# Head pairs 4 to 7 projected in float32 from the loaded tiles, and a new list of gates for the weight conversions

## The chip, the core and the metric

The kernel runs on one core of one Trainium2 chip. The core has five engines that run side by side, each with its own in-order queue of instructions: TensorE (PE in the profile, with its weight loads as PEld) does matrix products, VectorE (DVE), ScalarE (ACT) and GpSimd (POOL) do elementwise work, and SyncE (SP) issues most of the transfers (DMAs). Results of TensorE land in PSUM, everything else lives in SBUF. The metric is the device time of one execution in microseconds (us), as the median of several runs.

## The reference

Eight batches, each with 8 heads of 576 tokens and 64 numbers per token and head, go through an attention with a feature map, and the result through a token mix and a channel mix.

```python
def phi(x):
    proj = np.einsum('bhsd,df->bhsf', x, w_phi)          # 64 -> 128 features
    proj = proj - np.max(np.abs(proj), axis=-1, keepdims=True)
    return np.concatenate([np.exp(proj), np.exp(-proj)], axis=-1)
q_p, k_p = (phi(q), phi(k))
kv = np.einsum('bhsf,bhsd->bhfd', k_p, v)
z = np.sum(k_p, axis=2)
num = np.einsum('bhsf,bhfd->bhsd', q_p, kv)
den = np.einsum('bhsf,bhf->bhs', q_p, z)[..., None] + 1e-06
x = (num / den), heads side by side                       # (8, 576, 512)
h = np.maximum(xt @ w_tok1, 0.0) @ w_tok2                 # xt: tokens last, 576 -> 256 -> 576
u = x + h.transpose(0, 2, 1)
h2 = np.maximum(u @ w_ch1, 0.0) @ w_ch2                   # 512 -> 1536 -> 512
return u + h2
```

## The kernel before, in words

A head pair is two neighbouring heads of a batch; there are 32, pairs 0 to 3 are batch 0, pairs 4 to 7 batch 1. For each pair `keys()` projects the keys in five groups (four of two 128-row units, one of a single unit), subtracts the largest absolute value of each row, takes both exponentials and adds their products with the values in PSUM (`add_kv`). `queries()` does the same projection for the queries in one tail unit and four groups, turns the result, takes the exponentials and forms numerators and denominators. The projections of one pair are 18 units: 9 for keys and 9 for queries.

A projection is done in one of two ways by `less_max`. For pairs below `PLAIN` (4) it is a float32 product of the loaded tile (keys in the lower, queries in the upper 64 partitions) with `wz`, the projection weights beside zeros, 128 columns; VectorE then reads the result in PSUM twice, for the maximum (L252) and for the subtraction (L254). From pair 4 on `stack` first makes of the loaded `raw` tile a float32r stack of a rounded part (VectorE cast, L212) and a remainder (GpSimd subtraction, L213), two pieces of 512 and 640 columns for the keys and two for the queries; one float32r product of 256 columns per unit (L238) gives two partial sums; ScalarE copies one out (L245), VectorE adds the other (L247) and takes the maximum from SBUF (L252), and GpSimd subtracts it (L254).

The large products are done in float32r with each operand split in a rounded part and a remainder, three products for one. The channel weights arrive as 64-bit floats: 12 pieces of `wc1` and 12 of `wc2`. `convert` turns one piece: a DMA into a `raw` tile (SyncE), an absolute value on ScalarE (L146), four VectorE instructions on the bits (L147 to L150, tiles `bitsc`), a rounding copy on ScalarE and a subtraction on GpSimd (L77). The first eight conversions are gated: `turn_of` lets conversion n be written into the program only when `GATES[n]` denominators of batch 0 exist, and a copy of one column by GpSimd (L145) makes it wait for that denominator (`dn`, L443) on the chip. Each pair of batch 0 gives two such denominators, so gates 0 and 1 belong to pair 0, 2 and 3 to pair 1, and so on. The channel mix of a block of 256 tokens (`h` up, `acc` down) starts on a piece of the weights when that piece is in `loaded`.

Five generators (keys, queries, token mix, weight loading, channel mix) are woven by shares (`weave`), and a scheduler then sets each engine's order with a timeline of its own when the program is built. On the chip each engine follows that order strictly.

Of the kernel before, what the change touches and what calls it, by code (L numbers as in the profile page):

```python
# [18 lines left out]
B, H, S, D = 8, 8, 576, 64  # L19
NP = H // 2  # L20
# [2 lines left out]
T = 256  # L23
E = 1536
NC_, NE, NT = C // P, E // P, T // P
PLAIN = 4
ROWS = 8
BURST = 8
GATES = [4, 4, 6, 6, 7, 7, 7, 7]
BORROWED = 18  # L30
STAGES = 4
LAST = 15
# [12 lines left out]
def mixer_kernel(ctx, tc, qk, vm, vt, w_phi, w1, w2, wc1, wc2d, out):  # L45
# [21 lines left out]
    def column(pool, n, **kw):  # L67

        return pool.tile([P, 32], F32, **kw)[:, :n]
# [45 lines left out]
    for j in range(2):  # L115
        t = cst.tile([P, 672], F32, name=f"v{j}")[:, :650].rearrange("p (u j d) -> p u j d", u=5, j=2)
# [39 lines left out]
    def turn_of():  # L156
# [3 lines left out]
        ngated[0] += 1  # L160
        g = GATES[min(n, len(GATES) - 1)]
        yield from until(lambda: len(gates) > g)
        return gates[g] if n < len(GATES) else None

# [40 lines left out]
    def stack(raw, base, name):  # L205

        out = []
        lo = D - base
        for k, (c, n) in enumerate(((0, 512), (512, 640))):
            t = wk.tile([P, n], F32R, tag=f"{name[0]}{k}", name=f"st{name}{k}", bufs=1)  # L210
            src = raw[base:base + D, c:c + n]
            nc.vector.tensor_copy(t[base:base + D], src)  # L212
            nc.gpsimd.tensor_tensor(t[lo:lo + D], src, t[base:base + D].bitcast(F32), op=ALU.subtract)  # L213
            out.append(t)
        return out

    def less_max(ts, units, name, base=None):

        n, kind = len(units), name[0]
        if base == D:
            ps = ps_a.tile([P, 2, 2, F], F32, tag=f"a{nplain['k'] % 2}", name=f"pp{name}")
            nplain["k"] += 1
        elif base == 0 and (nplain["q"] % 2 == 0 or nplain["q"] >= BORROWED):
            ps = ps_h.tile([P, 2, 2, F], F32, tag="h", name=f"pp{name}")
            nplain["q"] += 1
        elif base == 0:
            ps = ps_w.tile([P, 2, 2, F], F32, tag="keys", name=f"pp{name}", bufs=1)
            nplain["q"] += 1  # L230
        elif kind == "k":
            ps = ps_w.tile([P, 2, 2, F], F32, tag="keys", name=f"pp{name}", bufs=1)
        else:
            ps = ps_w.tile([P, 2, 2, F], F32, name=f"pp{name}", **REST)
        for i, u in enumerate(units):
            t, c = (ts[1], 512) if u is None else (ts[u[0]], P * u[1])
            if base is None:
                nc.tensor.matmul(ps[:, i].rearrange("p two f -> p (two f)"), t[:, c:c + P],  # L238
                                 wp2.rearrange("p two f -> p (two f)"), start=True, stop=True)
            else:  # L240
                rows = slice(D, P) if name == "k0_0" else slice(0, P)
                nc.tensor.matmul(ps[:, i, 0], t[rows, c:c + P], wz[rows, base // D], start=True, stop=True)
        if base is None:
            part = wk.tile([P, 2, F], F32, tag="part", name=f"part{name}")
            nc.scalar.copy(part[:, :n], ps[:, :n, 1])  # L245
            pr = wk.tile([P, 2, F], F32, tag="p", name=f"p{name}")
            nc.vector.tensor_tensor(pr[:, :n], ps[:, :n, 0], part[:, :n], op=ALU.add)  # L247
            pr, eng = pr[:, :n], nc.gpsimd
        else:
            pr, eng = ps[:, :n, 0], nc.vector  # L250
        mx = column(wk, 2, tag=f"mx{kind}", name=f"mx{name}")
        nc.vector.tensor_reduce(mx[:, :n], pr, axis=AX.X, op=ALU.max, apply_absolute_value=True)  # L252
        pm = wk.tile([P, 2, F], F32, tag=f"pm{kind}", name=f"pm{name}", bufs=1 if kind == "t" else 2)
        eng.tensor_tensor(pm[:, :n], pr, mx[:, :n].unsqueeze(2).to_broadcast([P, n, F]), op=ALU.subtract)  # L254
        return pm

    nplain = {"k": 0, "q": 0}
    raws, pairs, kvs, loaded = {}, {}, {}, set()
    asked, attended, mixed = set(), set(), set()

    def load(i):

        raw = wk.tile([P, 2 * S], F32, tag="raw", name=f"raw{i}", bufs=1)
        lo, hi = (D if i <= PLAIN else 0), (D if i == B * NP else P)
        nc.sync.dma_start(raw[lo:hi], qk[i, lo:hi])
        raws[i] = raw

    def load_plain(i):

        out = []  # L270
        for k, (c, n) in enumerate(((0, 512), (512, 640))):
            t = wk.tile([P, n], F32, tag=f"{'kq'[i % 2]}{k}", name=f"pair{i}{k}", bufs=1)
            nc.sync.dma_start(t[D:], qk[i, D:, c:c + n])
            out.append(t)
        for k, (c, n) in enumerate(((0, 512), (512, 640))):
            nc.sync.dma_start(out[k][:D], qk[i + 1, :D, c:c + n])
        pairs[i] = out

    def keys():
        groups = [[(0, 0), (0, 1)], [(0, 2), (0, 3)], [(1, 0), (1, 1)], [(1, 2), (1, 3)], [None]]  # L280
        todo = None
        for i in range(B * NP):
            yield from until(lambda: i < 2 or i - 2 in asked)
            if i < PLAIN:
                load_plain(i)
            else:
                load(i)
            v_sb, queue = vtiles[i % 2], nc.sync if i else nc.scalar
            queue.dma_start(v_sb[:, 0:4].rearrange("p u j d -> p (u j) d")[:, :, :D], vm[i])
            for j in range(2):  # L290
                queue.dma_start(v_sb[j * D:(j + 1) * D, 4, j, :D], vt[i, j])
            plain = D if i < PLAIN else None
            ts = pairs[i] if i < PLAIN else stack(raws[i], D, f"k{i}")
            for g, us in enumerate(groups):
                pm = less_max(ts, us, f"k{i}_{g}", plain)
                kp = wk.tile([P, 2, 2, F], F32, tag="kp", name=f"kp{i}_{g}")
                for sg in range(2):
                    nc.scalar.activation(kp[:, :len(us), sg], pm[:, :len(us)], AF.Exp, scale=1.0 - 2.0 * sg)  # L298
                yield 0.22
                if todo:  # L300
                    add_kv(*todo)
                    yield 0.82
                todo = (i, g, us, kp, v_sb)
        add_kv(*todo)
        yield 0.82
# [40 lines left out]
    def queries():  # L346
        turned, split_up, row_major = None, None, None
        pieces = [(i, k, j) for i in range(B * NP) for k in range(2) for j in range(2)] + [None] * 3
        for piece in pieces:
            if row_major:  # L350
                flip(*row_major)
                yield 0.2
            row_major = None
            if split_up:
                yield from until(lambda: split_up[0] in kvs)
                if split_up[0] < ROWS:
                    row_major = row_numerators(*split_up)
                else:
                    numerators(*split_up)
                yield 0.75  # L360
            split_up = None
            if turned:
                split_up = turn(*turned)
                yield 0.25
            turned = None
            if piece:
                i, k, j = piece
                if (k, j) == (0, 0):
                    plain = 0 if i < PLAIN else None
                    if i < PLAIN:  # L370
                        yield from until(lambda: i in pairs)
                        ts = pairs[i]
                    else:
                        yield from until(lambda: i + 1 in raws or i + 1 == B * NP)
                        if i + 1 == B * NP:
                            load(i + 1)
                        ts = stack(raws[i + 1], 0, f"q{i}")
                    asked.add(i)
                    tail = less_max(ts, [None], f"t{i}", plain)
                    yield 0.11  # L380
                pm = less_max(ts, [(j, 2 * k), (j, 2 * k + 1)], f"q{i}_{k}{j}", plain)
                turned = (i, k, j, pm, tail)
                yield 0.22

# [99 lines left out]
    def until(cond):  # L484
        while not cond():
            yield None
# [129 lines left out]
    def token_stream():  # L616
        for b in range(B):
            for h in range(2):
                yield from until(lambda: b * NP + 2 * h + 1 in attended and (b > 0 or PLAIN - 1 in kvs))
                yield from token_mix(b, h, xts[b])  # L620
            mixed.add(b)

# [68 lines left out]
```

## Time and profile before

| | |
|---|---|
| device time, median of 3 runs | 1167.94 us (1167.78 to 1168.32) |
| the profiled execution: device time | 1168.64 us |
| the profiled execution: span, first to last instruction | 1166.6 us |
| busy: PE, DVE, POOL, ACT | 1121.0, 824.1, 573.7, 496.7 us |
| granted TensorE clock, mean | 0.985 of full speed |

The span is the time from the first instruction to the last in one profiled execution; the device time of that execution holds 2.04 us around it. Busy time of an engine counts its instructions; the matmuls of PE are pipelined and overlap, so its rate is better read from how many instructions it starts in a stretch (the number behind the x) than from its busy share. A float32 product of PE leaves two records in the trace, a float32r product one. The clock row shows in tenths what share of full speed TensorE was granted in each of 40 slices of the span.

### The profile page before, as it was taken

How to read it: one execution, taken by the hardware profiler on the slowest of the kernel's cores; microseconds unless marked ns; L12 is line 12 of the kernel's file. 1: busy time of each engine (PE TensorE's matmuls, PEld its weight loads, DVE VectorE, ACT ScalarE, POOL GpSimd, SP SyncE). 2: the span in 40 equal slices, each digit the busy share in tenths (PEclk: the TensorE clock that was granted, in tenths of full speed). 3: DMA queues.
4: the chain of work that ended last, by engine and by line, in shares of the span. 5: the costliest groups of instructions: out<-in, count | busy, mean ns of one | idle time of the engine just before them, and what ended most of it. 6: DMA issues, size and time to landing. Idle time of an engine off the chain costs nothing.

```text
span 1166.6 us, 24295 instructions
## 1 busy us (share of the span) xinstructions
PE 1121.0 (96%) x9208; PEld 1097.5 (94%) x9208; DVE 824.1 (71%) x1767; ACT 496.7 (43%) x1437; POOL 573.7 (49%) x727
## 2 busy tenths in 40 slices
PE   9997589999999999999999999999999999999998
PEld 8986489998999899999999999999999999999998
DVE  7689996458768777878878576684787878763111
ACT  5565454345444445444545343443443445431110
POOL 2266676257455555556646363563564665430000
PEclk9998599999999999999999999999999999999999
DMA  7433530111111111111111011110111110000000
GB/s 205 117 83 108 156 119 14 37 43 38 31 50 31 28 34 39 32 50 31 32 49 32 20 31 48 32 49 10 41 41 41 36 46 12 19 1 19 19 19 19
DMA packets 65460, 54.39 MB, mean 47 GB/s; under 512 B 44800, under 2 KB 56576, under 8 KB 65344
## 3 DMA queue, kind: packets, MB, share of 16 engines
q1 hardware_dynamic: 63824, 52.41, 15.6%
q8 instruction: 73, 1.20, 0.4%
q10 hardware_dynamic: 1520, 0.43, 0.2%
q14 instruction: 43, 0.35, 0.1%
HBM read 43.38 MB, written 9.44 MB: 45 GB/s over the span
## 4 chain that ended last, share of the span: by engine, by line
PE 81%; DVE 12%; issue 3%; POOL 2%; ACT 2%; DMA 0%; DVEq 0%; ACTq 0%; POOLq 0%
PE h L83 25%; PE acc L83 24%; PE pkv L323 9%; PE pn L83 6%; PE ph L83 3%; PE pa L83 3%; PE pt L392 3%; PE ppk L238 2%; PE ppq L238 2%; PE pr L430 1%; DVE bitsc L149 1%; DVE bitsc L147 1%; DVE qh L76 1%; PE px L504 1%; DVE bitsc L150 1%
## 5 line engine op out<-in xcount | busy, mean ns | idle before, releaser
L83 PE MATMUL acc<-gh,wc 128*128 128x256 f32 x1728 | 345.3, 284 | 2.4 <-ACT gh L570 2.4
L83 PEld LDWEIGHTS acc<-gh,wc 128*128 128x128 f32 x1728 | 275.9, 188 | 3.2 <-ACT gh L570 3.1
L83 PE MATMUL h<-uh,wc_h 128*128 128x256 f32 x864 | 247.0, 286 | 3.0 <-DVE gl L571 2.9
L83 PE MATMUL h<-uh,wc_l 128*128 128x256 f32 x864 | 246.0, 285 | 0.0
L83 PE MATMUL h<-ul,wc_h 128*128 128x256 f32 x864 | 244.2, 283 | 0.3 <-POOL ul L551 0.3
L83 PE MATMUL acc<-gl,wc 128*128 128x256 f32 x864 | 242.2, 282 | 0.0
L298 ACT ACTIVATE kp<-pmk 128x256 f32<-128x256 f32 (+1 forms) x320 | 109.0, 389 | 159.8 <-POOL pmk L254 148.6
L83 PEld LDWEIGHTS h<-uh,wc_h 128*128 128x128 f32 x864 | 163.6, 190 | 4.5 <-DVE gl L571 2.7
L323 PE MATMUL pkv<-v,kp 128*128 128x65 f32 (+2 forms) x1152 | 159.6, 271 | 7.5 <-ACT kv L332 4.8
L83 PEld LDWEIGHTS h<-ul,wc_h 128*128 128x128 f32 x864 | 163.8, 190 | 0.6 <-POOL ul L551 0.5
L83 PEld LDWEIGHTS h<-uh,wc_l 128*128 128x128 f32 x864 | 163.4, 189 | 0.0
L83 PEld LDWEIGHTS acc<-gl,wc 128*128 128x128 f32 x864 | 162.7, 188 | 0.1
L323 PEld LDWEIGHTS pkv<-v,kp 128*128 128x128 f32 x1152 | 148.8, 192 | 9.7 <-ACT kv L332 5.6
L77 POOL TENSOR_TENSOR ql<-qf,qh 128x320 fp32r<-128x320 f32 (+1 forms) x96 | 88.0, 917 | 103.9 <-DVE qh L76 90.0
L571 DVE SCALAR_TENSOR_TENSOR gl<-h,gh 128x512 fp32r<-128x512 f32 x108 | 73.6, 681 | 87.4 <-ACT gh L570 86.7
L399 ACT ACTIVATE qf<-pt 128x320 f32<-128x320 f32 (+1 forms) x256 | 91.9, 412 | 83.8 <-PE pt L392 69.7
L76 DVE CAST qh<-qf 128x320 fp32r<-128x320 f32 (+1 forms) x192 | 90.6, 488 | 36.1 <-ACT qf L399 30.6
L570 ACT ACTIVATE gh<-h 128x512 fp32r<-128x512 f32 x108 | 65.0, 601 | 117.9 <-PE h L83 116.4
L213 POOL TENSOR_TENSOR stq<-raw,stq 64x512 fp32r<-64x512 f32 (+1 forms) x56 | 83.1, 1484 | 54.8 <-DVE stq L212 45.6
L254 POOL TENSOR_TENSOR pmk<-pk,mxk 128x256 f32<-128x256 f32 (+1 forms) x140 | 85.6, 612 | 37.6 <-DVE mxk L252 33.8
L254 POOL TENSOR_TENSOR pmq<-pq,mxq 128x256 f32<-128x256 f32 x112 | 72.0, 643 | 61.0 <-DVE mxq L252 58.0
L213 POOL TENSOR_TENSOR stk<-raw,stk 64x512 fp32r<-64x512 f32 (+1 forms) x56 | 80.7, 1441 | 43.3 <-DVE stk L212 33.8
(122 smaller groups left out, 2366.9 us busy)
## 6 DMA issues: line engine op xcount, KB each, us to landing
raw<-in_qk SPq DMA_DIRECT2D x27, 576.0 KB, 3.7
rawc<-in_wc SPq DMA_DIRECT2D x24, 512.0 KB, 3.7
v<-in_vm SPq DMA_DIRECT2D x31, 256.0 KB, 3.3
out_x<-xt SPq DMA_DIRECT2D x12, 256.0 KB, 2.1
out_x<-xt SPq DMA_DIRECT2D x16, 192.0 KB, 2.0
raw<-in_w SPq DMA_DIRECT2D x8, 256.0 KB, 4.4
out_x<-xt SPq DMA_DIRECT2D x16, 128.0 KB, 1.8
pair<-in_qk SPq DMA_DIRECT2D x8, 160.0 KB, 4.5
```

Source lines behind the costliest of these rows:

```text
L76: eng_hi.tensor_copy(hi, raw)
L77: eng_lo.tensor_tensor(lo, raw, hi.bitcast(F32), op=ALU.subtract)
L83: nc.tensor.matmul(o, a, m, start=first and i == 0, stop=last and i == 2, skip_group_check=group_ok)
L213: nc.gpsimd.tensor_tensor(t[lo:lo + D], src, t[base:base + D].bitcast(F32), op=ALU.subtract)
L238: nc.tensor.matmul(ps[:, i].rearrange("p two f -> p (two f)"), t[:, c:c + P], wp2.rearrange("p two f -> p (two f)"), start=True, stop=True)
L254: eng.tensor_tensor(pm[:, :n], pr, mx[:, :n].unsqueeze(2).to_broadcast([P, n, F]), op=ALU.subtract)
L298: nc.scalar.activation(kp[:, :len(us), sg], pm[:, :len(us)], AF.Exp, scale=1.0 - 2.0 * sg)
L323: nc.tensor.matmul(o, kp[:, n, sg], v, start=g == 0 and n == 0 and sg == 0, stop=u is None, skip_group_check=True)
L392: nc.tensor.transpose(ptr[:, n], r, ident)
L399: nc.scalar.activation(full, src, AF.Exp, scale=1.0 - 2.0 * sg)
L570: nc.scalar.activation(gh, ph, AF.Relu)
L571: nc.vector.scalar_tensor_tensor(gl, ph, 0.0, gh.bitcast(F32), op0=ALU.max, op1=ALU.subtract)
```

## The change

Pairs below `PLAIN` = 8 now take the float32 way: pairs 4 to 7 are loaded by `load_plain` in four DMAs instead of one, and `stack` (L212, L213), the copy (L245) and the addition (L247) of these four pairs are gone; the maximum and the subtraction read PSUM, both on VectorE. The PSUM banks stay as they were: a new argument `early` gives the banks of the early pairs to pairs 0 to 3 alone. The list of gates is lower: the first conversion waits for the first denominator of pair 1 and no longer of pair 2. The condition of `token_stream` reads `NP - 1`, which has the value that `PLAIN - 1` had.

```diff
-PLAIN = 4
+PLAIN = 8
-GATES = [4, 4, 6, 6, 7, 7, 7, 7]
+GATES = [2, 3, 4, 5, 6, 6, 7, 7]
...
-    def less_max(ts, units, name, base=None):
+    def less_max(ts, units, name, base=None, early=False):
...
-        if base == D:
+        if early and base == D:
             ps = ps_a.tile([P, 2, 2, F], F32, tag=f"a{nplain['k'] % 2}", name=f"pp{name}")
...
-                pm = less_max(ts, us, f"k{i}_{g}", plain)
+                pm = less_max(ts, us, f"k{i}_{g}", plain, i < NP)
...
-                    tail = less_max(ts, [None], f"t{i}", plain)
+                    tail = less_max(ts, [None], f"t{i}", plain, i < NP)
...
-                yield from until(lambda: b * NP + 2 * h + 1 in attended and (b > 0 or PLAIN - 1 in kvs))
+                yield from until(lambda: b * NP + 2 * h + 1 in attended and (b > 0 or NP - 1 in kvs))
```

The first place is VectorE's queue behind the first denominator of pair 1 (`dn1_0`), where pairs 2 and 3 are projected (`mxk3` is the maximum of pair 3's keys, `pmk3` the subtraction, `bitsc1_0_0` the first piece of `wc1`). Before:

```order
L443 TENSOR_SCALAR dn1_0_549<-pr1_0_506 128x4
...
L252 TENSOR_REDUCE mxk3_1_701<-ppk3_1_698 128x2
L252 TENSOR_REDUCE mxk3_2_756<-ppk3_2_753 128x2
L445 TENSOR_TENSOR rows0_0_361<-pr1_0_506,dn1_0_549 64x128
L254 TENSOR_TENSOR pmk3_1_703<-ppk3_1_698,mxk3_1_701 128x256
L254 TENSOR_TENSOR pmk3_2_758<-ppk3_2_753,mxk3_2_756 128x256
L252 TENSOR_REDUCE mxq2_10_724<-ppq2_10_721 128x2
L212 CAST stk40_862<-raw4_857 64x512
```

and now:

```order
L443 TENSOR_SCALAR dn1_0_549<-pr1_0_506 128x4
...
L252 TENSOR_REDUCE mxk3_1_723<-ppk3_1_720 128x2
L147 TENSOR_SCALAR bitsc1_0_0_558<-bitsc1_0_0_558 128x512
L252 TENSOR_REDUCE mxk3_2_778<-ppk3_2_775 128x2
L445 TENSOR_TENSOR rows0_0_361<-pr1_0_506,dn1_0_549 64x128
L254 TENSOR_TENSOR pmk3_1_725<-ppk3_1_720,mxk3_1_723 128x256
L148 TENSOR_SCALAR bitsc1_0_0_558<-bitsc1_0_0_558 128x512
L254 TENSOR_TENSOR pmk3_2_780<-ppk3_2_775,mxk3_2_778 128x256
L252 TENSOR_REDUCE mxq2_10_746<-ppq2_10_743 128x2
L254 TENSOR_TENSOR pmq2_01_703<-ppq2_01_698,mxq2_01_701 128x256
L149 SCALAR_TENSOR_TENSOR bitsc1_0_0_558<-rawc1_0_0_556,bitsc1_0_0_558 128x512
```

The cast of pair 4's keys has gone, and the instructions of the first conversion stand among those of pairs 2 and 3; before, the first of them stood 32 instructions further on, behind the first denominator of pair 2.

The second place is SyncE's queue in the stage of the conversions (`raw6` and `pair60`, `pair61` bring pair 6 and its neighbour, `rawc` a piece of the channel weights, `v0` values). Before:

```order
L265 DMA raw6_1571<-in_qk 128x1152
L289 DMA v0_106<-in_vm 128x8x64
...
L138 DMA rawc1_2_512_1433<-in_wc1 128x512
L138 DMA rawc1_3_512_1464<-in_wc1 128x512
L138 DMA rawc2_4_1518<-in_wc2 128x512
L289 DMA v1_111<-in_vm 128x8x64
L265 DMA raw7_2117<-in_qk 128x1152
L138 DMA rawc2_5_1546<-in_wc2 128x512
```

and now:

```order
L138 DMA rawc2_4_1382<-in_wc2 128x512
L273 DMA pair60_1572<-in_qk 64x512
L276 DMA pair60_1572<-in_qk 64x512
L138 DMA rawc1_2_512_1301<-in_wc1 128x512
L138 DMA rawc1_3_512_1333<-in_wc1 128x512
L273 DMA pair61_1574<-in_qk 64x640
L276 DMA pair61_1574<-in_qk 64x640
L138 DMA rawc2_5_1410<-in_wc2 128x512
```

One load of a pair has become two steps of two loads, and pieces of the channel weights are queued between and behind them.

## Rows read from the trace of the kernel before

**Rows 1.** The page: the span, the busy times by engine, and of the 40 slices (29.2 us each) the busy tenths of PE and DVE and the granted clock in tenths.

```profile
span 1166.6 us, 24295 instructions
PE 1121.0 (96%) x9208; PEld 1097.5 (94%) x9208; DVE 824.1 (71%) x1767; ACT 496.7 (43%) x1437; POOL 573.7 (49%) x727
PE   9997589999999999999999999999999999999998
DVE  7689996458768777878878576684787878763111
PEclk9998599999999999999999999999999999999999
```

**Rows 2.** Busy time by stretch: the stretch and its length, then busy time and number of instructions of each engine, the granted clock, and the DMA share and rate.

```profile
0.00:62.00 62.00, 59.24 (x464) 55.16 (x464) 42.66 (x134) 34.07 (x96) 15.76 (x32) 1.00 0.60 156
40.00:60.00 20.00, 20.00 (x177) 19.31 (x176) 11.51 (x35) 10.27 (x31) 5.67 (x7) 1.00 0.19 54
62.00:188.00 126.00, 98.52 (x691) 90.48 (x691) 119.89 (x220) 66.64 (x168) 84.97 (x82) 0.86 0.34 106
120.00:140.00 20.00, 11.35 (x42) 9.21 (x42) 19.94 (x38) 9.41 (x22) 13.87 (x12) 0.50 0.49 150
260.00:300.00 40.00, 37.96 (x300) 36.02 (x299) 34.83 (x77) 19.55 (x59) 27.64 (x33) 1.00 0.16 43
188.00:1166.60 978.60, 963.25 (x8059) 951.86 (x8057) 661.50 (x1414) 396.02 (x1175) 472.94 (x613) 1.00 0.11 32
```

**Rows 3.** The chain of work that ended last, from 88 to 140 us (start, length, what).

```profile
114.44 1.34 DVE stk L212
116.30 1.60 issue
117.90 1.48 DVE bitsc L148
...
132.74 1.50 DVE bitsc L147
```

**Rows 4.** Who waited for whom from 62 to 188 us: in total, times, the longest.

```profile
PE ppk L238 <- DVE pk L247: 8.2, 4, 4.8
ACT bitsc L146 <- DMA rawc<-in_wc: 4.8, 3, 1.9
DVE bitsc L147 <- ACT bitsc L146: 2.6, 3, 1.2
```

**Rows 5.** The stretch from 62 to 188 us four times, busy time of the instructions of one tile or line alone: first the tile `bitsc` (DVE, ACT, POOL), then the casts L212 (DVE), the stack subtractions L213 (POOL), and the subtractions of the maximum L254 (DVE, POOL).

```profile
62.00:188.00 126.00, 78.84 (x95) 28.92 (x46) 34.19 (x29) 0.86 0.34 106
...
62.00:188.00 126.00, 12.27 (x13) 0.86 0.34 106
...
62.00:188.00 126.00, 20.18 (x13) 0.86 0.34 106
...
62.00:188.00 126.00, 1.23 (x3) 22.67 (x30) 0.86 0.34 106
```

**Rows 6.** The VectorE instructions of the tile `bitsc` by line: count, shortest, median and longest in ns, first and last start in us.

```profile
L147 DVE TENSOR_SCALAR bitsc<-bitsc x24: 395/726/1750, 62.6 to 184.8; 128x512 f32<-128x512 f32 x24
L148 DVE TENSOR_SCALAR bitsc<-bitsc x24: 407/502/1483, 63.2 to 185.6; 128x512 uint32<-128x512 uint32 x24
L149 DVE SCALAR_TENSOR_TENSOR bitsc<-rawc,bitsc x24: 674/698/1935, 64.5 to 186.3; 128x512 uint32<-128x512 uint32 x24
L150 DVE SCALAR_TENSOR_TENSOR bitsc<-rawc,bitsc x24: 671/685/1766, 66.7 to 188.0; 128x512 uint32<-128x512 uint32 x24
```

**Rows 7.** The maximum (L252) and the subtraction (L254) of the keys by what they read, `pk` in SBUF or `ppk` in PSUM, and VectorE's addition (L247) from 62 to 188 us (busy us, mean ns). The first three rows: count, shortest, median and longest in ns.

```profile
L252 DVE TENSOR_REDUCE mxk<-pk x140: 265/407/422, 59.4 to 1018.6; 128x2 f32<-128x256 f32 x112, 128x1 f32<-128x128 f32 x28
...
L252 DVE TENSOR_REDUCE mxk<-ppk x20: 271/406/423, 8.5 to 49.2; 128x2 f32<-128x256 f32 x16, 128x1 f32<-128x128 f32 x4
...
L254 DVE TENSOR_TENSOR pmk<-ppk,mxk x20: 276/406/425, 9.5 to 53.9; 128x256 f32<-128x256 f32 x16, 128x128 f32<-128x128 f32 x4
...
L247 DVE TENSOR_TENSOR pk<-ppk,partk 128x256 f32<-128x256 f32 x14 | 5.7, 410 | 0.3 <-ACT partk L245 0.3
```

**Rows 8.** PE's projections of keys by line over the whole span, L242 for pairs 0 to 3 and L238 for the other 28 (count, shortest, median and longest in ns).

```profile
L242 PE MATMUL ppk<-wz,pair x72: 272/275/373, 7.7 to 48.5; 128*128 128x128 f32 x68, 64*128 64x128 f32 x4
...
L238 PE MATMUL ppk<-wp,stk x252: 275/281/583, 58.1 to 1010.1; 128*128 128x256 f32 x126
```

**Rows 9.** The chain of work again, from 45 to 56 us, where PE works without a gap: float32 projections (two records each), and float32r products of 256 columns (one record each).

```profile
45.09 0.89 PE ppk L242 x8
...
50.80 1.41 PE pa L83 x12
```

**Rows 10.** The copies that hold the gates on GpSimd (first and last start), and VectorE's first denominators of pair 1 in order of time (start, length).

```profile
L145 POOL COPY bitsc<-dn x8: 177/180/642, 60.5 to 95.9; 128x1 f32<-128x1 f32 x8
...
44.04 0.16 DVE L443 TENSOR_SCALAR dn<-pr 128x4 f32<-128x4 f32 x1 [0.71 <-PE pr L430]
...
50.97 0.16 DVE L443 TENSOR_SCALAR dn<-pr 128x4 f32<-128x4 f32 x1
```

More of the change, by code (lines that the diff above doesn't have):

```diff
@@ L215, in stack @@
         return out
-    def less_max(ts, units, name, base=None):
+    def less_max(ts, units, name, base=None, early=False):
         n, kind = len(units), name[0]
-        if base == D:
+        if early and base == D:
             ps = ps_a.tile([P, 2, 2, F], F32, tag=f"a{nplain['k'] % 2}", name=f"pp{name}")
             nplain["k"] += 1
-        elif base == 0 and (nplain["q"] % 2 == 0 or nplain["q"] >= BORROWED):
+        elif early and base == 0 and (nplain["q"] % 2 == 0 or nplain["q"] >= BORROWED):
             ps = ps_h.tile([P, 2, 2, F], F32, tag="h", name=f"pp{name}")
             nplain["q"] += 1
-        elif base == 0:
+        elif early and base == 0:
             ps = ps_w.tile([P, 2, 2, F], F32, tag="keys", name=f"pp{name}", bufs=1)
@@ L378, in queries @@
                     asked.add(i)
-                    tail = less_max(ts, [None], f"t{i}", plain)
+                    tail = less_max(ts, [None], f"t{i}", plain, i < NP)
                     yield 0.11
-                pm = less_max(ts, [(j, 2 * k), (j, 2 * k + 1)], f"q{i}_{k}{j}", plain)
+                pm = less_max(ts, [(j, 2 * k), (j, 2 * k + 1)], f"q{i}_{k}{j}", plain, i < NP)
                 turned = (i, k, j, pm, tail)
```

## The prediction

> **What bounds the kernel now.** I read the page first: the span is 1166.6 us, PE is busy for 96% of it, and its weak slices after the start are the fourth to the sixth, where DVE stands at nine tenths and the granted clock of PE falls to half speed [rows 1]. By stretch the picture is sharp: from 188 us to the end PE starts 8059 instructions in 978.6 us, one per 0.121 us; from 62 to 188 us it starts 691 in 126 us, one per 0.182 us, while DVE is busy for 119.9 us of the 126 [rows 2]. [...] The chain in that stretch runs through DVE: bits of the weights and casts of the stacks [rows 3], and PE's longest waits for an engine are for DVE's addition [rows 4]. So before 188 us, when DVE ends the last conversion [rows 6], DVE is the bound; behind it PE is. Both parts of the change act here.
>
> **Landmark.** I take the end of the last conversion on DVE, 188.0 us, as the point to compare. PE has started 1152 instructions by then (464 and 691 by stretch, with a few counted twice). Counted in the changed kernel's PE queue, with two records for each float32 product, DVE's last conversion stands where PE has 1155 to 1184 behind it, say 1170, of 9280 instead of 9208. So 8110 are left instead of 8056, 54 more: 54 x 0.121 = 6.6 us that are paid behind the landmark. The gain is how much sooner the landmark comes, less 6.6 us.
>
> **PE's own cost.** 72 projections (4 pairs x 18) become 144 records for 72: the early pairs have 72 key records for 4 pairs, the others 252 for 28 [rows 8]. In a dense stretch 8 such records take 0.89 us, 0.111 each, and 12 float32r ones 1.41 us, 0.118 each [rows 9]. 144 x 0.111 - 72 x 0.118 = 7.5 us over the whole kernel. The part ahead of the landmark is hidden behind DVE while DVE is the bound there; if that cover goes, all 7.5 us are on the path.
>
> **DVE's work up to the landmark.** It was 119.9 us busy from 62 to 188 [rows 2].
> - Casts: 13 take 12.3 us [rows 5]. Twelve belong to the keys of pairs 5 to 7 and the queries of pairs 4 to 6 and go; one, of pair 8, stays. I put it at 0.5 us, an estimate: half of the mean of 12.3/13 = 0.94, as it is of the smaller size and POOL is freer.
> - Addition and subtraction: each group loses L247 (0.41 us) and gains L254 on DVE (0.41 us) [rows 7]. Nothing changes on DVE. The maximum reads PSUM instead of SBUF: medians 406 and 407 ns, nothing.
> - Conversions: 95 of the 96 DVE instructions of 24 pieces lie in the stretch, 78.8 us [rows 5], 3.3 us a piece. The order shows two pieces moved ahead of the second denominator of pair 2, among instructions that ran at 44 to 61 us; the first gate moves from 60.5 to behind 44.0 us, the second to behind 51.0 us [rows 10]. DVE was busy for 11.5 us of 20 from 40 to 60 us [rows 2], so 8.5 us of idle time cover two pieces (4.3 to 6.6 us). I charge 1 us for what does not fit. If that cover fails, all 6.6 us are paid by pairs 2 and 3, where PE had no gap.
> - 22 pieces are left. The shortest durations of the four instructions add up to 395+407+674+671 = 2.15 us [rows 6], against 3.3 on average; some are stretched to 1.9 us. POOL was busy for 85.0 us of the stretch [rows 2], a share of 0.67. The change takes away 22.7 us of subtractions and about 18.8 of the 20.2 us of stack remainders [rows 5], leaving some 41 us after the two moved pieces, a share near 0.4. If the stretch follows POOL's share, 3.3 - 2.15 = 1.15 shrinks to about 0.68: 2.8 us a piece. That no row shows directly; the bounds are 2.15 and 3.3.
> - The rest of DVE: 119.9 - 78.8 - 12.3 = 28.8 us, and 0.5 for the cast that stays, and 1.5 us because at the changed landmark pair 7 is three groups further (2.2) and the channel mix one block back (0.7): 30.8 us.
>
> Sum: 22 x 2.8 + 30.8 = 92.4 us. DVE's busy share was 0.95 in that stretch and 0.87 from 260 to 300 us [rows 2], where it is less crowded; I take 0.90: 103 us. The landmark comes at 62 + 1 + 103 = 166 us, 22 us sooner, and the gain is 22 - 6.6 = 15.4 us. Span 1151.2 us; with the 2.04 us around it 1153.2; the profiled run lies 0.7 us above the median, so 1152.5 us.
>
> [...]
>
> [...]
>
> **Rivals.**
> - PE becomes the bound at once. Conversions at 2.15 us give 22 x 2.15 + 30.8 = 78 us of DVE, 82 at a share of 0.95; PE needs 1170 - 448 (464 less the 16 of the warm-up) = 722 instructions from 62 us on, at 0.121 us 87 us. The landmark is at 62 + 87 = 149 to 150 us, the gain 38.5 - 6.6 = 32 us: 1136 us. For it: PE keeps 177 in 20 us from 40 to 60 us. Against it: the channel mix can't fill PE before its weights are there, and each projection waits for two DVE instructions in a strict order.
> - No relief. The conversions stay at 3.3 us: 73 + 30.8 = 103 us, at 0.87 119 us, landmark 182 us: a gain of 6 that the 6.6 us eat up, 1169 us. For it: POOL's subtraction of each piece stays and lies beside the next piece's bits. Against it: the longest stretches need a POOL instruction nearby, and 42 of POOL's 82 instructions there go (30 of L254, 12 of L213 [rows 5]).
> - Slower, by waits in DVE's queue. Every piece of weights needs its DMA, then ACT, then four DVE instructions that stand at a fixed place with pairs queued behind them. SP's queue now has two waiting steps for a pair where it had one, with pieces of weights between and behind them; a pair's tile is free only when the queries of the pair before last are projected. Before, DVE waited 3 times for ACT, 2.6 us in all, the longest 1.2, and ACT waited for DMA 4.8 us [rows 4]. If each of the 24 pieces waits 1.2 us, DVE needs 92.4/0.95 + 28.8 = 126 us, the landmark stays at 189 us, and the 6.6 us come on top: 1175 us. It turns the result at 0.9 us a piece. Against it: from a pair's release in DVE's order to the next piece's first instruction there are 15 to 20 DVE instructions, some 9 us, for a DMA of a few.
>
> **Chances.** The forecast (1146 to 1161 us) 0.50; PE bound at once 0.19; no relief 0.17; slower 0.14. This kernel's measurement tells 0.2% (2.3 us) from no change. Of "no relief" half falls within 0.2%, a bit more than a third of it on the faster side: faster 0.76, same 0.08, slower 0.16. The range runs from 1138 us, near the end of PE's case, to 1169 us, the end of "no relief"; the forecast's own is 1146 to 1161.
>
> **What would show it.** The last L150 of `bitsc` should start near 166 us (150 in PE's case, 182 or later without relief); the mean DVE time of a piece near 2.8 us; POOL near 0.4 busy in that stretch; the first L147 of `bitsc` near 46 us; PE's clock without a slice at half speed; behind the landmark one PE instruction per 0.121 us as before. The casts L212 and remainders L213 should fall from 112 to 96 each. I am wrong if waits of DVE for ACT or DMA grow beyond 20 us, if PE loses more than 2 us from 40 to 62 us, or if PE's rate behind the landmark changes.

## The result and the profile after

The changed kernel takes 1149.18 us (median of 4 runs, 1147.9 to 1151.3) where the kernel before took 1167.86 us beside it: a ratio of 0.984, with a 95% interval of 0.982 to 0.986. The forecast was 1152.5 us, in a range from 1138 to 1169. The profiled execution took 1147.9 us, 1.8 us more than its span.

The page of the changed kernel, the same lines as [rows 1]:

```profile
span 1146.1 us, 24296 instructions
PE 1117.9 (98%) x9280; PEld 1098.4 (96%) x9280; DVE 796.0 (69%) x1751; ACT 486.3 (42%) x1397; POOL 521.3 (45%) x671
PE   8998899999999999999999999999999999999998
DVE  7779873478687797887787685775777878663111
PEclk9999899999999999999999999999999999999999
```

PE has 72 more instructions and is yet 3.1 us less busy. In PE's row the weak fourth to sixth slices (7, 5, 8 before) now read 8, 8, 9. One slice of the clock is still below 9. The loss is smaller, not gone.

Busy time by stretch, with the columns of [rows 2] (length, then PE, PEld, DVE, ACT and POOL with their counts, the granted clock, the DMA share and rate):

```profile
0.00:62.00 62.00, 57.68 (x449) 53.31 (x450) 43.16 (x132) 33.89 (x95) 14.97 (x31) 1.00 0.63 170
40.00:62.00 22.00, 21.27 (x183) 20.29 (x183) 14.28 (x42) 12.34 (x36) 5.95 (x8) 1.00 0.44 124
62.00:165.00 103.00, 94.36 (x747) 89.71 (x746) 92.55 (x214) 59.58 (x143) 40.29 (x38) 0.95 0.40 123
62.00:188.00 126.00, 117.28 (x941) 112.31 (x939) 100.13 (x232) 68.15 (x167) 49.13 (x51) 0.96 0.34 105
100.00:120.00 20.00, 14.68 (x106) 13.54 (x104) 20.00 (x45) 11.81 (x26) 11.54 (x8) 0.91 0.59 189
120.00:140.00 20.00, 17.66 (x118) 16.17 (x118) 18.66 (x42) 11.47 (x28) 9.04 (x7) 0.83 0.54 174
0.00:164.60 164.60, 151.64 (x1190) 142.62 (x1191) 135.33 (x344) 93.47 (x237) 55.09 (x68) 0.97 0.48 140
0.00:188.00 188.00, 174.96 (x1387) 165.62 (x1387) 143.29 (x363) 102.04 (x261) 64.11 (x82) 0.97 0.44 127
164.60:1146.10 981.50, 966.23 (x8092) 955.80 (x8091) 660.62 (x1407) 392.83 (x1160) 466.19 (x603) 1.00 0.11 32
```

The gain can be read from PE's counter alone. At 188 us PE has started 1387 of 9280 instructions; before, 1152 of 9208. It then has 7893 left and not 8056: 163 fewer, at 0.1213 us each (981.5/8092) 19.8 us, of the 20.5 us by which the span is shorter. Next to nothing of it comes from behind 188 us. In the stretch from 120 to 140 us PE was granted a clock of 0.50 before and started 42 instructions; now it has 0.83 and 118. From 100 to 120 DVE is still busy without a gap.

The granted clock from 62 to 188 us rose from 0.86 to 0.96. In windows of 2 us from 60 to 188 us it reads either 1.00 or 0.50 in all but four of 64, in either kernel. By an estimate from the two means and these two levels, PE spent some 35 us of the 126 at 0.50 before and spends some 10 now. No run here separates what the clock gave back from what the shorter waits did.

The VectorE instructions of the tile `bitsc` by line (count, shortest, median and longest in ns, first and last start in us):

```profile
L147 DVE TENSOR_SCALAR bitsc<-bitsc x24: 399/419/1510, 46.7 to 161.0; 128x512 f32<-128x512 f32 x24
L148 DVE TENSOR_SCALAR bitsc<-bitsc x24: 409/416/1374, 48.1 to 161.4; 128x512 uint32<-128x512 uint32 x24
L149 DVE SCALAR_TENSOR_TENSOR bitsc<-rawc,bitsc x24: 668/684/1762, 49.5 to 162.9; 128x512 uint32<-128x512 uint32 x24
L150 DVE SCALAR_TENSOR_TENSOR bitsc<-rawc,bitsc x24: 674/686/1614, 50.9 to 164.6; 128x512 uint32<-128x512 uint32 x24
```

In [rows 6] the median L147 was 726 ns and its shortest 395; now the median is 419. Most instructions are no longer stretched, but the longest still are (1.4 to 1.8 us). The same tile alone, over the stretch that holds all 24 pieces (DVE, ACT, POOL), now and then in the kernel before:

```profile
0.00:210.00 210.00, 63.47 (x96) 30.29 (x48) 35.54 (x32) 0.98 0.40 116
```

```profile
0.00:210.00 210.00, 79.53 (x96) 30.28 (x48) 35.78 (x32) 0.92 0.40 113
```

63.47/24 = 2.64 us a piece now, 79.53/24 = 3.31 before.

The waits from 62 to 190 us (total, times, longest), which answer to [rows 4]:

```profile
ACT kp L298 <- DVE pmk L254: 12.0, 7, 3.4
...
ACT bitsc L146 <- DMA rawc<-in_wc: 4.6, 5, 1.4
...
PE ppk L242 <- DVE pmk L254: 3.5, 3, 2.4
...
DVE bitsc L147 <- ACT bitsc L146: 2.2, 2, 1.8
```

PE's wait for DVE fell from 8.2 to 3.5 us, and DVE's wait for ACT did not grow. ACT's wait is for the subtraction, which is now DVE's; PE is not behind it in this row. In the chain from 88 to 140 us (start, length) DVE's bits stand beside PE's own work, where [rows 3] had bits and casts:

```profile
115.90 1.68 DVE bitsc L149
...
118.51 1.53 DVE bitsc L150
...
122.06 2.52 PE pr L430 x12
124.57 2.01 PE pkv L323 x8
```

### The profile page after: what moved, and what is told of

Read it like the earlier page. It is cut to its first block, busy times and chain, and to the rows that moved or that the text cites. A ratio compares the mean times of both kernels' runs of the same rounds, so it can differ in the third digit from the quotient of the medians.

```text
span 1146.1 us, 24296 instructions
## 1 busy us (share of the span) xinstructions
PE 1117.9 (98%) x9280; PEld 1098.4 (96%) x9280; DVE 796.0 (69%) x1751; ACT 486.3 (42%) x1397; POOL 521.3 (45%) x671
## 4 chain that ended last, share of the span: by engine, by line
PE 84%; DVE 8%; DMA 2%; ACT 2%; POOL 2%; issue 1%; SPq 0%; DVEq 0%; POOLq 0%; ACTq 0%
PE h L83 25%; PE acc L83 25%; PE pkv L323 9%; PE pn L83 6%; PE ph L83 3%; PE pa L83 3%; PE pt L392 3%; PE pr L430 2%; PE ppk L238 2%; PE ppq L238 2%; DMA raw<-in_w 1%; DVE qh L76 1%; PE px L504 1%; PE ppq L242 1%; DVE bitsc L149 1%
## 5 line engine op out<-in xcount | busy, mean ns | idle before, releaser
L83 PE MATMUL pn<-qh,kv 128*128 128x320 f32 (+1 forms) x384 | 99.7, 298 | 0.2 <-DVE qh L76 0.2
L551 POOL TENSOR_TENSOR ul<-xt,uh 128x64 fp32r<-128x64 f32 (+3 forms) x120 | 60.0, 525 | 82.6 <-ACT uh L550 81.9
L479 DVE RECIPROCAL den<-den 128x320 f32<-128x320 f32 (+1 forms) x48 | 93.5, 1949 | 0.9
L213 POOL TENSOR_TENSOR stk<-raw,stk 64x512 fp32r<-64x512 f32 (+1 forms) x48 | 68.9, 1436 | 47.2 <-DVE stk L212 38.7
```

Of the source, the lines that this page charges most:

```text
L83: nc.tensor.matmul(o, a, m, start=first and i == 0, stop=last and i == 2, skip_group_check=group_ok)
L479: nc.vector.reciprocal(den, den)
L551: nc.gpsimd.tensor_tensor(l[:, d:d + n], t[:, c, o:o + n], h[:, d:d + n].bitcast(F32), op=ALU.subtract)
```

## The experiments

My theory was that VectorE's load and its stretching by GpSimd's work set the time up to the last conversion, and that the float32 way removes both. The rivals: that the earlier gates do it; that GpSimd's company costs nothing and only the casts matter; that it is the shorter way of a group (PSUM to one engine, with no copy on ScalarE). "Piece" is DVE's busy time of `bitsc`, divided by 24; "POOL" is GpSimd's busy share from 62 to 165 us.

| kernel | us | ratio to before, 95% | piece | POOL | last L150 starts |
|---|---|---|---|---|---|
| before | 1167.86 | | 3.31 | 0.68 | 188.0 |
| after | 1149.18 | 0.982 to 0.986 | 2.64 | 0.39 | 164.6 |
| e1: gates alone | 1169.13 | 1.000 to 1.002 | 3.27 | 0.72 | 181.1 |
| e2: float32 way alone | 1147.75 | 0.981 to 0.984 | 2.64 | 0.42 | 169.7 |
| e3: POOL remainders back | 1149.42 | 0.982 to 0.985 | 2.77 | 0.59 | 165.2 |
| e4: DVE casts back | 1155.68 | 0.988 to 0.991 | 2.54 | 0.38 | 169.5 |
| e5: POOL subtractions back | 1152.44 | 0.985 to 0.989 | 2.87 | 0.58 | 166.1 |
| e6: e3 and e5 | 1160.61 | 0.993 to 0.996 | 3.04 | 0.74 | 175.5 |
| e7: 12 pairs in float32 | 1153.68 | 0.986 to 0.989 | 2.64 | 0.39 | 163.6 |
| e8: longer way of a group | 1152.60 | 0.986 to 0.989 | 2.99 | 0.61 | 165.3 |
| e9: e6 and casts | 1173.94 | 1.003 to 1.007 | 2.92 | 0.74 | 190.3 |
| e10: after again | 1146.31 | 0.980 to 0.984 | 2.66 | 0.41 | 162.7 |
| e11: e2 again | 1147.51 | 0.981 to 0.984 | 2.64 | 0.41 | 170.5 |

The kernel before took 1167.7 to 1167.9 us beside all of them. The changed kernel was timed twice, at 1149.18 and (e10) 1146.31 us. What a run costs is given below against the first; against the second it is 2.9 us more. The share of 0.68 in the first row comes from this window of the kernel before:

```profile
62.00:165.00 103.00, 78.81 (x530) 71.46 (x529) 97.15 (x183) 53.71 (x136) 69.84 (x68) 0.83 0.38 118
```

### The two halves apart: e1 and e2

e1 is the kernel before with one line changed; e2 undoes that line in the changed kernel.

```diff
-GATES = [4, 4, 6, 6, 7, 7, 7, 7]
+GATES = [2, 3, 4, 5, 6, 6, 7, 7]
```

> Pairs 4 to 7 stay on the stacks; only the list of gates is the new one. Theory A (DVE sets the landmark, and the casts and the company of POOL are most of its load): the gates bring only the two pieces that move into idle time ahead of 62 us, so the landmark comes 4 to 6 us sooner than at 188 us and the time is 1162 to 1164 us. Rival B (the earlier start of the conversions is what counts): most of the 18.7 us, 1150 to 1154 us, and the landmark near 170 us. Rival C (the early conversions stand in the way of pairs 2 and 3): 1168 us or more.

> Pairs 4 to 7 in float32 from the loaded tiles; the list of gates is the old one. Theory A: the casts gone and a piece of weights at 2.6 to 2.8 us on DVE instead of 3.3, so the landmark comes near 171 us and the time is 1153 to 1156 us. Rival B: PE pays its 7.5 us for little, 1165 to 1170 us, landmark at 180 us or later.

e1 came out at 1169.13 us, 1.3 us above the kernel before, the time of rival C; e2 at 1147.75, 5 us below theory A's range, with the landmark (169.7 us) near the 171 of theory A. The gates bring no gain here, and the float32 way is worth all of it. Yet e1 did end its conversions 6.9 us sooner, more than theory A had said. The windows of e1, up to that landmark and behind it:

```profile
0.00:181.10 181.10, 150.84 (x1099) 138.82 (x1100) 156.85 (x351) 98.48 (x260) 101.92 (x112) 0.92 0.43 127
181.10:1167.80 986.70, 970.93 (x8112) 959.99 (x8110) 662.89 (x1418) 397.66 (x1177) 473.72 (x615) 1.00 0.11 32
```

and of the kernel before up to the same time, and in the 7 us that follow:

```profile
0.00:181.10 181.10, 150.86 (x1092) 138.74 (x1093) 155.78 (x344) 96.98 (x255) 96.62 (x111) 0.91 0.44 127
...
181.00:188.00 7.00, 7.00 (x64) 7.00 (x63) 6.87 (x10) 3.82 (x10) 4.21 (x4) 1.00 0.01 2
```

By 181.1 us DVE had been busy for 156.9 and 155.8 us, and PE had started 1099 and 1092 instructions. Lower gates put the conversions ahead of other DVE work; they make neither less nor denser work of it. And in the kernel before, PE was full from 181 to 188 us while DVE still converted, so these last 7 us were not lost and there was nothing in them to win.

### What GpSimd's company costs: e3, e5 and e6

e3 adds to the changed kernel the remainders of pairs 4 to 7 on GpSimd (unread, from the loaded tiles):

```diff
+    def ghost(ts, base, name):
+        for k, c, n in ((0, 0, 256), (0, 256, 256), (1, 0, 320), (1, 320, 320)):
+            s = streamed(wk, [P, SEG[0][1]], F32R, tag="qh", name=f"gh{name}{k}{c}")
+            src = ts[k][base:base + D, c:c + n]
+            nc.gpsimd.tensor_tensor(s[D - base:P - base, :n], src, src, op=ALU.subtract)
...
+            if NP <= i < PLAIN:
+                ghost(ts, D, f"k{i}")
...
+                        if i >= NP:
+                            ghost(ts, 0, f"q{i}")
```

> The changed kernel, and for pairs 4 to 7 GpSimd does subtractions of the size of the stack remainders again (in pieces of 256 and 320 columns, into a tile that nobody reads); DVE gets no cast. Theory A (a piece of weights is stretched on DVE by POOL's company): a piece takes 2.9 to 3.1 us on DVE instead of 2.6, the landmark moves from 164.6 to 170 to 174 us and the time is 1154 to 1159 us. Rival D (the stretch is DVE's own affair, or idle engines cost nothing): 2.6 us a piece, and 1147 to 1151 us as before.

e5 adds, behind DVE's subtraction in each group of pairs 4 to 7, the same subtraction on GpSimd, unread:

```diff
+        if base is not None and not early:
+            s = wk.tile([P, 2, F], F32, tag="p", name=f"again{name}")
+            nc.gpsimd.tensor_tensor(s[:, :n], pm[:, :n], mx[:, :n].unsqueeze(2).to_broadcast([P, n, F]),
+                                    op=ALU.subtract)
```

> The changed kernel, and behind each subtraction of the maximum of pairs 4 to 7 GpSimd does one of the same size again, from SBUF into a tile that nobody reads; the remainders had no effect, so of the removed GpSimd work these are what is left to test. Theory A (company of POOL stretches the conversions): a piece takes 2.9 to 3.2 us on DVE, PE has started about 1330 instructions by 188 us instead of 1375 to 1390, and the time is 1154 to 1159 us. Rival D (POOL's work costs nothing here): 2.6 to 2.8 us a piece and 1147 to 1151 us.

e6 has both edits.

> The changed kernel with both kinds of GpSimd work of pairs 4 to 7 put back as unread copies, remainders and subtractions. Theory A: POOL is as full as in the kernel before (share near 0.67), a piece takes 3.2 to 3.4 us as there, and the time is 1157 to 1163 us. Rival D: 1148 to 1152 us; then the gain comes from the casts and from the shorter way from a projection to its exponential, and not from the conversions.

One alone cost little: 0.2 us for e3 against after's 1149.18, 3.3 for e5. Both together cost 11.4. Of the forecasts, e3's time and landmark (165.2 us) came out as rival D had them, with pieces (2.77 us) between the two; e5's time lies between the two ranges; e6's time is in theory A's range, its pieces (3.04 us) are shorter than theory A said. The count of PE's instructions tells the same as the times. Up to 188 us, for e3, e5, e6 and the second execution of the changed kernel, e10, in turn:

```profile
0.00:188.00 188.00, 173.33 (x1376) 164.05 (x1377) 146.41 (x362) 101.92 (x260) 89.21 (x114) 0.97 0.44 126
```

```profile
0.00:188.00 188.00, 172.27 (x1360) 162.94 (x1361) 146.86 (x357) 99.73 (x255) 83.91 (x113) 0.97 0.43 125
```

```profile
0.00:188.00 188.00, 165.97 (x1286) 156.28 (x1287) 148.41 (x354) 96.61 (x245) 103.95 (x137) 0.95 0.43 124
```

```profile
0.00:188.00 188.00, 174.20 (x1401) 164.75 (x1402) 145.56 (x366) 102.55 (x262) 63.46 (x83) 0.99 0.44 127
```

Against the 1387 and 1401 of the changed kernel's two executions, e3 has 11 to 25 fewer, e5 27 to 41, e6 101 to 115: together more than the sum of the two, by either. The tile `bitsc` alone in e3, e5 and e6 in turn, one kernel to a fence:

```profile
0.00:210.00 210.00, 66.39 (x96) 30.46 (x48) 35.42 (x32) 0.98 0.40 116
```

```profile
0.00:210.00 210.00, 68.81 (x96) 30.48 (x48) 33.58 (x32) 0.98 0.40 116
```

```profile
0.00:210.00 210.00, 72.89 (x96) 30.63 (x48) 35.27 (x32) 0.96 0.40 116
```

The pieces need 2.9, 5.3 and 9.4 us more of DVE than in the changed kernel (63.47): nearly additive here (8.2 against 9.4). The time is not. e6's waits from 62 to 190 us show what grew (the projections are in L249 there, the subtraction in L261), and its engines from 115 to 120 us stand below them:

```profile
PE ppk L249 <- DVE pmk L261: 11.4, 4, 5.2
...
DVE bitsc L147 <- ACT bitsc L146: 9.7, 6, 3.8
...
ACT bitsc L146 <- POOL bitsc L145: 3.7, 3, 2.4
...
115.00:120.00 5.00, 0.16 (x1) 0.16 (x1) 5.00 (x10) 1.65 (x4) 3.34 (x5) 0.72 0.33 105
```

At a POOL share of 0.74 DVE waits for ACT 9.7 us instead of 2.2, and PE's projections wait for DVE 11.4 us instead of 3.5. ACT's 3.7 us of waiting for the small gate copies L145 in GpSimd's queue are one part of it, and not the main one: the last of these copies starts at 91.8 us, and PE's longest wait for DVE (5.2 us) ends at 119.8 us, in a stretch in which DVE was busy without a gap and PE started one instruction. Waits in DVE's queue, which the rival "slower" named, do grow at this share; which of them makes the time grow is not shown. The first 3 to 5 us of stretching cost 0.2 to 3.3 us; the next 4, with these waits, cost 8. A caution: an unread subtraction also reads `pm` and the maximum, so that by the program these come free later in e5 and e6; whether some of DVE's waits there come from that is not shown.

By the spans in the traces of the two kernels, the stretching lies beside GpSimd's instructions. Before, 24 of the 96 VectorE instructions of `bitsc` overlap none of GpSimd's, and none of these 24 is more than 25 ns above the shortest of its line; the 49 that are more than 50 ns above it all overlap one, and the longest reaches 1.9 us. In the changed kernel 63 of the 96 overlap none (at most 29 ns above the shortest), and the 21 that are more than 50 ns above it all overlap one. The maxima (L252) of the kernel before do not stretch: up to 190 us none of 71 takes more than 0.43 us, 31 of them beside a GpSimd instruction. More GpSimd work went with longer pieces (2.64 us in the changed kernel, 2.77, 2.87 and 3.04 with one and with both kinds of GpSimd work put back), but the share alone does not set the price: in e3 and e5 nearly the same share (0.59 and 0.58) gave 2.77 and 2.87, and the kernel before had 3.31 at 0.68.

### What the casts cost: e4

```diff
-            nc.gpsimd.tensor_tensor(s[D - base:P - base, :n], src, src, op=ALU.subtract)
+            nc.vector.tensor_copy(s[base:base + D, :n], src)
```

The edit is to e3's helper: the casts of pairs 4 to 7 come back on VectorE, unread.

> The changed kernel, and for pairs 4 to 7 DVE does casts of the size of the stack casts again (in pieces of 256 and 320 columns, into a tile that nobody reads); POOL gets nothing. Theory A (DVE is the bound up to the landmark): 32 casts of 0.3 to 0.4 us, about 11 us of DVE, move the landmark to 172 to 176 us and the time to 1156 to 1161 us. Rival E (PE is the bound already and DVE has room): within 3 us of 1149 us.

Measured 1155.68 us, 6.5 us above the changed kernel and just under theory A's range; the landmark came at 169.5 us and not at 172 to 176. The casts (L222 there) alone from 62 to 188 us, and then all of e4's engines up to 165 us and up to 188 us:

```profile
62.00:188.00 126.00, 10.29 (x24) 0.96 0.35 105
...
62.00:165.00 103.00, 91.48 (x715) 86.31 (x715) 94.01 (x230) 58.09 (x142) 39.49 (x38) 0.95 0.42 128
...
0.00:188.00 188.00, 170.02 (x1337) 159.88 (x1338) 150.76 (x391) 100.81 (x260) 62.73 (x82) 0.97 0.45 124
```

10.3 us of DVE work cost 6.5 us of time, about 0.6 us for each. In part it was made up for: the pieces were shorter (2.54 us), and up to 188 us DVE was busy for 7.5 us more than in the changed kernel (150.76 against 143.29). The 2.9 us of longer pieces in e3 cost 0.2 us against the first timing of the changed kernel and 3.1 against the second. Whether DVE time costs more in casts than in longer pieces stays open.

### All of the load back: e9

e9 has e5's edit, and in e3's helper the casts and the remainders computed from them, with the short way of a group kept.

```diff
-            nc.gpsimd.tensor_tensor(s[D - base:P - base, :n], src, src, op=ALU.subtract)
+            nc.vector.tensor_copy(s[base:base + D, :n], src)
+            nc.gpsimd.tensor_tensor(s[D - base:P - base, :n], src, s[base:base + D, :n].bitcast(F32), op=ALU.subtract)
```

> The changed kernel with all the work of the stacks put back as unread copies: casts on DVE, each followed by its remainder on GpSimd, and a subtraction on GpSimd behind each maximum. What is then still gone is only the way of the data: no group waits for that work. If the loads act one by one, 1149.2 + 6.5 (casts) + 11.4 (both kinds of POOL work) = 1167 us; if they add to each other as the two kinds of POOL work did, 1170 us or more. If the shorter way of a group were most of the gain: below 1163 us.

Measured 1173.94 us, 6.2 us above the kernel before, as forecast for loads that add to each other. Its windows, and then its casts (L222 there) and its remainders (L223) alone:

```profile
62.00:165.00 103.00, 85.44 (x569) 78.79 (x568) 91.90 (x205) 50.16 (x122) 75.89 (x85) 0.82 0.36 117
...
0.00:188.00 188.00, 166.69 (x1219) 155.08 (x1220) 156.87 (x381) 93.90 (x238) 108.83 (x133) 0.90 0.42 124
...
0.00:188.00 188.00, 17.27 (x32) 0.90 0.42 124
...
0.00:188.00 188.00, 29.99 (x32) 0.90 0.42 124
```

The casts (L212) and the remainders (L213) of the kernel before up to the same time:

```profile
0.00:188.00 188.00, 13.19 (x15) 0.91 0.43 122
...
0.00:188.00 188.00, 23.01 (x15) 0.91 0.43 122
```

Of the gain nothing is left, though the short way of a group is kept: without the load taken off DVE and GpSimd it wins nothing. What it is worth beside that relief is not shown. By the prediction's estimate of PE's own cost, 1167.7 + 7.5 = 1175.2 against 1173.9 leaves it 1.3 us, but this is no upper bound: e9 has more load than the kernel before, 17.3 us of casts for 13.2 and 30.0 of remainders for 23.0, and DVE waits for ACT 8.8 us from 62 to 190 us where it waited 2.6. Its granted clock from 62 to 165 us is 0.82, near the 0.83 of the kernel before, where e4 had 0.95 and e6 0.92; how much of e9's time is the clock's was not tried.

### A longer way: e8, and more pairs: e7

e8 sends the groups of pairs 4 to 7 over a copy on ACT; DVE takes the maximum from SBUF and GpSimd subtracts.

```diff
-        else:
+        elif early:
             pr, eng = ps[:, :n, 0], nc.vector
+        else:
+            pr = wk.tile([P, 2, F], F32, tag="p", name=f"p{name}")
+            nc.scalar.copy(pr[:, :n], ps[:, :n, 0])
+            pr, eng = pr[:, :n], nc.gpsimd
```

> The changed kernel, but for pairs 4 to 7 ScalarE copies the projection to SBUF, DVE takes only the maximum from there and GpSimd subtracts: 36 instructions or 14 us less on DVE, 36 more on ACT and POOL, and the way of a group is longer by two engines. If DVE's load is what counts (11 us of casts cost 6.5 us): 1140 to 1145 us. Rival F (the length of the way from projection to exponential counts, or POOL's company): 1153 to 1162 us.

Measured 1152.60 us: slower by 3.4 us than the changed kernel, between the two ranges. The engines from 62 to 165 us:

```profile
62.00:165.00 103.00, 91.86 (x711) 86.12 (x710) 88.89 (x173) 66.09 (x171) 62.72 (x67) 0.93 0.38 119
```

DVE has 41 instructions fewer than in the changed kernel, but is only 3.7 us less busy. A piece is at 2.99 us, which takes 8.4 us more over all 24: more than half of the 14 us that the subtractions freed. PE has started 36 instructions fewer by then. The run changes DVE's load, GpSimd's load and the length of the way at once and does not tell them apart.

e7 takes four more pairs the float32 way.

```diff
-PLAIN = 8
+PLAIN = 12
```

> Pairs 8 to 11 too in float32 from the loaded tiles: 72 more records for PE where PE is the bound, and casts, additions and POOL work of four more pairs gone where they cost nothing. By the sum of the prediction: 72 x 0.121 = 8.7 us on the path, less what is hidden, so 1155 to 1159 us. Rival (DVE and POOL relief still pays behind the conversions): 1145 to 1151 us.

Measured 1153.68 us, below the forecast range: slower by 4.5 us than after's 1149.18 and by 7.4 than its second timing, for 72 more PE records. The window behind 188 us:

```profile
188.00:1152.00 964.00, 949.76 (x7961) 941.20 (x7960) 639.98 (x1374) 374.09 (x1098) 413.86 (x536) 1.00 0.11 31
```

By 188 us e7 had started 1393 records against 1387, so nearly all 72 fall behind it, where PE is the bound and there is no DVE time to win. The price is near PE's own cost of the prediction (7.5 us) or below it.

### The two fastest again: e10 and e11

> The changed kernel once more, beside the next one on the same chip, to tell the two lists of gates apart: 1149 us. If the early conversions cost PE something from 40 to 62 us and bring nothing, it is 1 to 2 us above the next one.

> The new pairs with the old list of gates once more: 1147 to 1148.5 us if the lower gates cost 1 to 2 us; 1149 us or more if they bring nothing or something.

Both are the kernels as they were, timed once more: 1146.31 and 1147.51 us, where the first timing gave 1149.18 and 1147.75. The order turned round, so the two can't be told apart, and no kernel tried here is faster than either.

## Why the prediction was right, and where not

- **DVE as the bound, PE behind it.** Right. PE's rate behind the landmark was 0.1213 us per instruction, as before, and the gain came from before 188 us. The first L147 of `bitsc` started at 46.7 us (46 forecast), and no slice of the clock stands at half speed.
- **The landmark.** 164.6 us for 166. The window from 62 to 165 us had 92.55 us of DVE work for the forecast sum of 92.4, and a share of 0.90 as taken. Two terms inside that sum were off and cancel, so that the sum came out so close by luck. The pieces took 2.64 us instead of 2.8 (22 x 0.16 = 3.5 us less). The rest of DVE took 92.55 - 58.0 (the `bitsc` part) = 34.55 us instead of 30.8: from 62 us to its landmark DVE had done 38 maxima where the kernel before had done 33 to its own, so 5 more groups of two instructions of 0.41 us, 4.1 us, where I had allowed 2.2 for three. The other two stood ahead of 62 us before (38 maxima there, 36 now). What else is in the 34.55 was not followed.
- **GpSimd's share near 0.4.** Right (40.29/103 = 0.39).
- **The gates, "8.5 us of idle time cover two pieces".** This step fell. From 40 to 62 us the two pieces took 5.15 us of DVE, but DVE was busy for only 1.0 us more than before (14.28 against 13.29): some 4 us of other DVE work no longer stand there. The kernel before, and then the tile `bitsc` in the changed kernel:

```profile
40.00:62.00 22.00, 22.00 (x194) 21.31 (x193) 13.29 (x43) 12.23 (x37) 6.51 (x9) 1.00 0.20 54
```

```profile
40.00:62.00 22.00, 5.15 (x8) 2.60 (x4) 2.89 (x4) 1.00 0.44 124
```

I let the two pieces moved ahead lower the bound by 6.6 us, less 1 us that does not fit, some 6 us of landmark at a share of 0.90. The landmark did move by 6.9 us in e1, and the time got 1.3 us longer. A moved landmark is only a gain if PE has done as much by then, and in e1 PE had 8109 instructions left there (9208 less 1099), not 8056: 53 x 0.121 = 6.4 us, nearly all of it. In the change the sum stayed right because it counted what PE had left at the new landmark (8110). The measured 8090 is 20 fewer: 2.4 us, beside 1.4 us of landmark, of the 5.1 us by which the span beat the forecast; the rest is the rate, 0.1213 us for 0.1215. Without the gates (e2) the landmark came at 169.7 us with 1250 instructions started, 8030 left: a later landmark, and the same time.
- **PE's loss from 40 to 62 us.** 183 instructions for 194: 11 x 0.121 = 1.3 us, under the 2 us named. Over the whole start PE lost 15 (449 for 464), 1.8 us, but four of them ahead of 40 us, before the first piece's first instruction at 46.7 us, and in e10 only 5 (459). So 1.3 us is the better figure for what the two pieces cost pairs 2 and 3.
- **Stretching follows POOL's share.** The size was close, but no run shows a stretch in proportion to the share, from which the sum has its 2.8 us: between e3, e5, e6, e8 and e9 a piece takes 2.77 to 3.04 us at shares of 0.58 to 0.74, not in order of the share. Scaled as I did, 0.59 would have given 3.2 and 0.74 3.4.
- **Addition for subtraction, and the maximum from PSUM, at nothing.** The rows bear the size out, and answer to [rows 7]:

```profile
L252 DVE TENSOR_REDUCE mxk<-ppk x40: 273/411/425, 7.7 to 162.7; 128x2 f32<-128x256 f32 x32, 128x1 f32<-128x128 f32 x8
...
L254 DVE TENSOR_TENSOR pmk<-ppk,mxk x40: 263/414/426, 8.6 to 163.5; 128x256 f32<-128x256 f32 x32, 128x128 f32<-128x128 f32 x8
```

The maximum from PSUM has a median of 411 ns, against 407 for the form from SBUF in [rows 7]: a difference of 4 ns, about 0.1 us over 36 maxima.
- **Rivals.** "PE bound at once" did not come: DVE was still busy for 20.00 of the 20 us from 100 to 120. "No relief" fell with 2.64 us a piece. "Slower, by waits" stayed out of the change (DVE waited 2.2 us for ACT); such waits showed in e6 and e9 (9.7 and 8.8 us), where GpSimd's share was 0.74.

How the 18.7 us divide is shown only roughly: putting GpSimd's work back costs 11.4 us and the casts 6.5, near the whole by sum, but all together cost 24.8, with PE's own cost never taken out. The parts depend on each other, and the shorter way of a group and the clock are not separated from them.

## What to carry to other kernels

A landmark on one engine measures a gain only together with what the bound engine behind it has left; count that engine's instructions at one fixed time in both traces. In this case instructions moved within a full queue won nothing (e1: 1.3 us above the kernel before); those taken off it did (e4: 10.3 us of casts put back cost 6.5), and load taken off a neighbour that stretches it counted too (e6: 3.04 us a piece for 2.64). The last spare tenths of the helper engine were worth the most here: either of two additions to GpSimd cost 0.2 to 3.3 us (3.1 to 6.1 by the second timing), both cost 11 (14).

## What the runs showed that I had not expected

- Two extra loads on GpSimd cost 0.2 and 3.3 us alone, 11.4 us together, and 3.1, 6.1 and 14.3 against the second timing.
- The same changed kernel took 1149.18 and 1146.31 us in two timings (the kernel before: within 0.2 us), more than the 0.2% taken as the limit. The profiles differ from 120 to 140 us: a granted clock of 0.83 and 118 PE instructions in the first, and in e10

```profile
120.00:140.00 20.00, 17.05 (x134) 15.41 (x134) 17.90 (x39) 11.86 (x30) 9.74 (x8) 1.00 0.61 190
```

In the 20 us ahead of it both have thin PE work at the same clock (14.68 and 13.80 us busy, 0.91). Whether the clock falls again behind such a stretch thus differs from one execution to another; 16 instructions are 1.9 us, near the 2.1 us between the two profiled executions. What decides it stays open.
